# Keys and queries scaled by one instruction each, a chunk's tokens in another order, and x at one place modulo 512 bytes

## The chip, the cores and the metric

The kernel runs on one core of a Trainium2 chip. The metric is the device time of one execution in microseconds (us); lower is better. Engines are named as in the profile: PE is TensorE's matmul, PEld its weight load, DVE VectorE, ACT ScalarE, POOL GpSimd, SP the engine that issues most DMAs.

## The reference

A gated linear attention is followed by two feed-forward layers, all in float32:

```python
# q, k, v, f_logit: (4, 8, 768, 48)
f = 1 / (1 + exp(-f_logit))
for t in range(768):
    state = f[:, :, t, :, None] * state + einsum('bhd,bhe->bhde', k[:, :, t], v[:, :, t])
    y[:, :, t] = einsum('bhd,bhde->bhe', q[:, :, t], state)
x = y.transpose(0, 2, 1, 3).reshape(3072, 384)
h = maximum(x @ w_in1, 0);  x = (h * h) @ w_out1          # 384 -> 2048 -> 384
h = x @ w_in2;  x = where(h > 0, h, exp(minimum(h, 0)) - 1) @ w_out2
```

## The kernel before

**Attention.** The 3072 tokens are 24 groups of 128 (6 chunks of 4 batches; groups 0 to 3 have no carried state). A group's `ff`, `qk` and v tiles hold all 8 heads: two heads on 112 partitions (`ROWS`), four such pairs (`NP`) along the free dimension. `a_decay` makes the products of the gates with two scans on VectorE, outward from the middle of the chunk: `ds[.., 0, ..]` holds the decays of the outward scan, `ds[.., 1, ..]` their counterparts from the scan in the other direction, in runs of 65 elements for each half chunk of 64 tokens. `a_scale` multiplies keys and queries by them, in four instructions of 112x256: each half of the 64-token halves takes its factors from the one or the other scan. The two for k run on GpSimd (L158, L159), the two for q on VectorE (L161, L162), for groups 1 to 3 on GpSimd. Keys lie in the order `outward` (tokens 63 to 0, then 64 to 127), queries in plain order, so one of the four reads its factors backwards. `a_scores` (transposes and scores on TensorE), `a_mask` (VectorE, `copy_predicated` with `msk`), `a_state`, `a_direct` or `a_out` follow, and `a_hi` and `a_lo` write a group's result into x as a rounded part `xh` and a rest `xl`.

**Layers.** Tokens go in 12 blocks of 512, six for each layer (blocks 0 to 5 and 6 to 11), and the 2048 hidden units in 16 slices f. A unit is one (block, slice). `up` makes ph with nine matmuls of 128x512, six with `xh` and three with `xl` (L354). `between` makes gh and gl on ScalarE, VectorE and GpSimd, and `down`, two units later, adds nine matmuls into y (L406), three times gh, gh, gl. So TensorE's order in a unit is xh x6, xl x3, then (gh, gh, gl) x3. Weights of the first layer are decoded from 64-bit words on ScalarE and VectorE (L51, L53, L56, L57) and split in two parts (L323, L324), one slice a unit, ahead of use.

**Order.** Everything is scheduled by hand. `START` lists the first steps, one letter and a number each: f, q, v, r load, g is `a_gate`, d `a_decay`, c `a_scale`, s `a_scores`, t `a_transposed`, m `a_mask`, k `a_state`, y `a_direct`, h `a_hi`, l `a_lo`, w and W decode and split weights, U, B, L are `up`, `between`, `low`. After it the loop over units runs, and `plan` puts the steps of groups 4 to 23 and the weights in front of the `up` of a unit. The steps of a group stand in consecutive units: gate, decay, scale, then scores (block 1) or one unit of pause and scores (later blocks).

**Places.** Pools lie one behind the other in each partition's memory: `one`, `two`, `three`, `wpool`; a pool holds its tags in the order of their first use, each in as many buffers as the pool has (sizes rounded up to 32 bytes). In `two` there are ff, qk, then the two buffers of `xh` and the two of `xl`, then raw, vk, dec, gg, wc, x1; gh, gl and yo are in `three`, the weights in `wpool`. Block 0 takes the second buffer of `xh` and `xl` (the first holds a padded v then), block 1 the first, and so on in turn. An x tile has 3 x 512 + 16 elements, 6208 bytes, and x itself starts 64 bytes into it; 6208 is 64 more than 12 x 512. Tiles of gh, gl (2048 bytes) and weights (6144) are multiples of 512. If r is where xh of the odd blocks starts, modulo 512, then xh of the even blocks starts at r+64, xl of the odd ones at r+128, xl of the even ones at r+192, and gh, gl and the weights, 54,528 bytes behind the first, at r+256.

Of the kernel before, what the change touches and what calls it, by code (L numbers as in the profile page):

```python
# [11 lines left out]
F32 = mybir.dt.float32  # L12
F32R = mybir.dt.float32r
# [17 lines left out]
BLOCKS = [(layer, sum(n[:i]), n[i]) for layer, n in enumerate(SIZES) for i in range(len(n))]  # L31


START = """f0 q0 f1 I q1 M v0 f2 v1 f3 g0 q2 d0 q3 c0 g1 v2 d1 s0 r0 c1 r1 t0 g2 k0 g3 m0 y0 d2 c2 h0 v3 s1 t1
d3 m1 v4 k1 s2 c3 w0 t2 k2 s3 l0 y1 m2 q4 t3 m3 W0 r2 h1 k3 w1 f4 y2 h2 y3 l1
l2 h3 l3 W1 g4 r3 w2 U0 B0 L0 W2 d4 U1 B1 L1 w3 r4"""
FIRST = (0, 3, 6, 8), (-6, -2, 2, 6)
STAGED = 15
DMIN = 2.0**-52


# [18 lines left out]
def chunked(ctx, tc, ff, qk, vk, vz, wraw, mask, ident, flag, out):  # L60
# [8 lines left out]

    one = ctx.enter_context(tc.tile_pool(name="one", bufs=1))  # L70
    two = ctx.enter_context(tc.tile_pool(name="two", bufs=2))
    three = ctx.enter_context(tc.tile_pool(name="three", bufs=3))
    wpool = ctx.enter_context(tc.tile_pool(name="wpool", bufs=NF))
    dram = ctx.enter_context(tc.tile_pool(name="dram", bufs=1, space=bass.MemoryType.DRAM))
# [10 lines left out]
    ss = [one.tile([128, 2, NP, 128], F32, name=f"ss{i}") for i in range(2)]  # L85
    state = [one.tile([ROWS, NP, 48], F32, name=f"state{b}") for b in range(B)]
    dlast = [one.tile([ROWS, NP], F32, name=f"dlast{b}") for b in range(B)]
    x2d = dram.tile([NK, 128, NT], F32, name="x2d")
    wst = dram.tile([NF, 128, 2, 2, DM], F32, name="wst")

# [62 lines left out]
            G.tensor_copy(dlast[g % B], here[:, :, 1])  # L153

    def a_scale(g):
        dt, gt = (ds[g % 2][:, o, o:o + 520].rearrange("r (p h l) -> r p h l", h=2, l=65) for o in range(2))
        q, k = (st[g]["qk"][:, o].rearrange("r (p h l) -> r p h l", h=2, l=64) for o in range(2))
        G.tensor_tensor(out=k[:, :, 0], in0=k[:, :, 0], in1=dt[:, :, 0, 0:64], op=ALU.mult)  # L158
        G.tensor_tensor(out=k[:, :, 1], in0=k[:, :, 1], in1=gt[:, :, 1, 1:65], op=ALU.mult)  # L159
        E = G if 0 < g < B else V  # L160
        E.tensor_tensor(out=q[:, :, 1], in0=q[:, :, 1], in1=dt[:, :, 1, 1:65], op=ALU.mult)  # L161
        E.tensor_tensor(out=q[:, :, 0], in0=q[:, :, 0], in1=gt[:, :, 0, 63::-1], op=ALU.mult)  # L162

    def a_scores(g):
        s = st[g]
# [97 lines left out]

    def new_x(i):
        n = BLOCKS[i][2]
        tiles = [two.tile([128, NK * n + 16], F32R, tag=f"x{p}", name=f"x{p}{i}") for p in "hl"]
        xr[i] = tuple(t[:, 16:].rearrange("r (k t) -> r k t", t=n) for t in tiles)

    def a_hi(g):
        i, o = where[g]  # L270
# [224 lines left out]
def general(ctx, tc, nat, wraw, ident, out):  # L495

    nc = tc.nc
    V, A, G, PE = nc.vector, nc.scalar, nc.gpsimd, nc.tensor
    T = 384
    one = ctx.enter_context(tc.tile_pool(name="g_one", bufs=1))  # L500
    ps = ctx.enter_context(tc.tile_pool(name="g_ps", bufs=1, space=PSUM))
    dram = ctx.enter_context(tc.tile_pool(name="g_dram", bufs=1, space=bass.MemoryType.DRAM))
    yd = dram.tile([2 * B, NP, D, 2, T], F32, name="yd")

    sel = one.tile([ROWS, 2], F32, name="sel")
    vb = one.tile([ROWS, S], F32, name="vb")
    V.memset(sel, 0.0)
    V.memset(sel[0:48, 0:1], 1.0)
    V.memset(sel[64:112, 1:2], 1.0)
    V.memset(vb, 0.0)  # L510
    with tc.For_i(0, B, 1) as b:
        with tc.For_i(0, NP, 1) as p:
            fqk = one.tile([ROWS, 3, S], F32, name="fqk")
            for c in range(3):
                nc.sync.dma_start(out=fqk[:, c], in_=nat[bass.ds(b, 1), bass.ds(p, 1), c].rearrange("b p r s -> (b p r) s"))
            f = fqk[:, 0]
            V.tensor_scalar(out=f, in0=f, scalar1=-80.0, scalar2=None, op0=ALU.max)
            A.activation(f, f, AF.Exp, scale=-1.0)
            V.tensor_scalar(out=f, in0=f, scalar1=1.0, scalar2=None, op0=ALU.add)
            V.reciprocal(out=f, in_=f)  # L520
            with tc.For_i(0, D, 1) as e:
                for j, (lo, hi) in enumerate(HD):
                    src = nat[bass.ds(b, 1), bass.ds(p, 1), 3, bass.ds(e + 64 * j, 1)].rearrange("b p r s -> (b p r) s")
                    nc.sync.dma_start(out=vb[lo:hi], in_=src.to_broadcast([hi - lo, S]))
                kv = one.tile([ROWS, S], F32, name="g_kv")
                V.tensor_tensor(out=kv, in0=fqk[:, 2], in1=vb, op=ALU.mult)
                V.tensor_tensor_scan(out=kv, data0=f, data1=kv, initial=0.0, op0=ALU.mult, op1=ALU.add)
                V.tensor_tensor(out=kv, in0=kv, in1=fqk[:, 1], op=ALU.mult)
                y = one.tile([2, S], F32, name="g_y")
                for h in range(2):  # L530
                    yp = ps.tile([2, T], F32, name=f"g_yp{h}")
                    PE.matmul(yp, sel, kv[:, T * h:T * h + T], start=True, stop=True)
                    A.activation(y[:, T * h:T * h + T], yp, AF.Copy)
                    nc.sync.dma_start(
                        out=yd[bass.ds(2 * b + h, 1), bass.ds(p, 1), bass.ds(e, 1)].rearrange("n p e j t -> (n p e j) t"),
                        in_=y[:, T * h:T * h + T],
                    )
    x = one.tile([128, NK, T], F32, name="g_x")
    acc = one.tile([128, NK, T], F32, name="g_acc")

    with tc.For_i(0, 2, 1) as h, tc.For_i(0, B, 1) as b:
        y = yd[bass.ds(2 * b + h, 1)].rearrange("n p e j t -> (n p) e j t")
        for k in range(NK):
            for j in range(2):
                nc.sync.dma_start(out=x[64 * j:64 * j + 48, k], in_=y[k, :, at_(k, j)])
                nc.sync.dma_start(
                    out=x[64 * j + 48:64 * j + 64, k], in_=y[NP - 1, 16 * k:16 * k + 16, at_(NP - 1, j)]
                )
        for layer in range(2):
            V.memset(acc, 0.0)  # L550
            with tc.For_i(0, NF, 1) as ff:
                raw = one.tile([128, 2 * DM], I64, name=f"g_raw{layer}")
                nc.sync.dma_start(out=raw, in_=wraw[layer, bass.ds(ff, 1)].rearrange("f p m -> (f p) m"))
                w = one.tile([128, 2 * DM], U32, name=f"g_w{layer}")
                decode(nc, raw, w)
                w = w.bitcast(F32)
                ph = ps.tile([128, T], F32, name=f"g_ph{layer}")
                for k in range(NK):
                    PE.matmul(ph, w[:, 128 * k:128 * k + 128], x[:, k], start=(k == 0), stop=(k == NK - 1))
                g = one.tile([128, T], F32, name=f"g_g{layer}")  # L560
                if layer == 0:
                    A.activation(g, ph, AF.Relu)
                    A.activation(g, g, AF.Square)
                else:
                    A.activation(g, ph, AF.Relu, scale=-1.0)
                    th = one.tile([128, T], F32, name="g_t")
                    A.activation(th, g, AF.Tanh, scale=-0.5)
                    A.activation(g, g, AF.Exp, scale=-1.0)
                    V.scalar_tensor_tensor(out=g, in0=g, scalar=1.0, in1=th, op0=ALU.add, op1=ALU.mult)
                    V.scalar_tensor_tensor(out=g, in0=ph, scalar=0.0, in1=g, op0=ALU.max, op1=ALU.add)  # L570
                for m in range(NK):
                    py = ps.tile([128, T], F32, name=f"g_py{m % 2}")
                    PE.matmul(py, w[:, DM + 128 * m:DM + 128 * m + 128], g, start=True, stop=True)
                    V.tensor_tensor(out=acc[:, m], in0=acc[:, m], in1=py, op=ALU.add)
            V.tensor_copy(x, acc)
        for k in range(NK):
            dst = out[k].rearrange("p (h c b t) -> p h c b t", h=2, c=NC // 2, b=B)[:, bass.ds(h, 1), :, bass.ds(b, 1)]
            nc.sync.dma_start(
                out=dst.rearrange("p h c b t -> p (h c b) t"), in_=x[:, k].rearrange("p (c t) -> p c t", t=128)
            )  # L580


# [12 lines left out]
def _layout(q, k, v, f_logit, moe_w_in, moe_w_out, moe2_w_in, moe2_w_out):  # L595
# [9 lines left out]

    ff = np.full((NG, ROWS, 521), -64.0, np.float32)
    ff[:, :, :520].reshape(NG, ROWS, 2 * NP, 65)[:, :, :, 1:] = heads(f_logit, outward, 8.0).reshape(NG, ROWS, 2 * NP, 64)
    qk = np.stack([heads(q, fwd, 0.0), heads(k, outward, 0.0)], axis=2)
    vk = v.reshape(B, NP, 2, NC, 128, D)[:, :, :, :, outward].transpose(3, 0, 4, 1, 2, 5).reshape(NG, 128, DM)
    vz = np.zeros((B, 128, NK, 2, 112), v.dtype)  # L610
    vp = vk[:B].reshape(B, 128, NP, 2, D)
# [18 lines left out]
    for c, a in enumerate((f_logit, q, k, v)):  # L630
        nat[:, :, c, :, :D] = a.reshape(B, NP, 2, S, D).transpose(0, 1, 2, 4, 3)
    nat = nat.reshape(B, NP, 4, 128, S)[:, :, :, :ROWS]
    mask = (outward[:, None] <= fwd[None, :]).astype(np.int32)
    return {
        "ff": ff, "qk": qk, "vk": vk, "vz": vz, "nat": nat, "wraw": wraw, "mask": mask,
        "ident": np.eye(128, dtype=np.float32),
# [14 lines left out]
```

## Time and profile before

| what | value |
|---|---|
| median of 3 timed runs | 930.47 us (927.55 to 930.67) |
| profiled execution, its own time | 927.88 us |
| its span, first to last instruction | 926.1 us |
| mean granted TensorE clock | 0.990 |
| PE busy | 897.8 us (97%) |
| DVE, ACT, POOL busy | 564.7, 441.5, 359.6 us |

The span is what the trace shows; 1.78 us of the execution's time lie outside it. Busy shares are means over stages that differ, so they say which engine is the fullest, not where time can be won.

### The profile page before, as it was taken

The numbers are of one execution on the slowest core, as the hardware profiler recorded it, in microseconds if no ns is written. First come the engines' busy times: TensorE is split into PE (matmuls) and PEld (weight loads), VectorE is DVE, ScalarE is ACT, GpSimd is POOL, SyncE is SP. The second block draws the span as 40 slices with busy tenths as digits, with TensorE's granted clock in tenths as the row PEclk, the third lists the DMA queues.
The fourth block names the chain that finished last, engine by engine and source line by source line (L and its number), as shares of the span: only waits on it lengthen the run. The fifth ranks groups of instructions, "written<-read, shape, count | busy, mean of one in ns | idle before, by whom it ended". The sixth has DMA issues, their size and how long they took to land.

```text
span 926.1 us, 13344 instructions
## 1 busy us (share of the span) xinstructions
PE 897.8 (97%) x5001; PEld 724.5 (78%) x5001; DVE 564.7 (61%) x834; ACT 441.5 (48%) x751; POOL 359.6 (39%) x294
## 2 busy tenths in 40 slices
PE   6798899999999999999999999999999999999996
PEld 4676688878888887777888888888888888888885
DVE  8999977677676776774301356555555565555543
ACT  4477655444444544444444444444444544444443
POOL 5322425555565455553232233233332333323321
PEclk8999999999999999999999999999999999999999
DMA  8456434334344533433256510100100100100001
GB/s 282 143 177 196 134 107 144 109 110 144 111 140 138 189 112 109 145 112 112 103 189 221 201 38 1 57 12 1 58 11 1 57 12 1 57 12 5 31 1 38
DMA packets 30792, 88.46 MB, mean 96 GB/s; under 512 B 4992, under 2 KB 9728, under 8 KB 30720
## 3 DMA queue, kind: packets, MB, share of 16 engines
q1 hardware_dynamic: 28848, 77.32, 25.0%
q10 hardware_dynamic: 1872, 10.22, 3.2%
q8 instruction: 40, 0.66, 0.3%
q14 instruction: 32, 0.26, 0.1%
HBM read 64.52 MB, written 22.02 MB: 93 GB/s over the span
## 4 chain that ended last, share of the span: by engine, by line
PE 89%; DVE 7%; issue 1%; ACT 1%; POOL 1%; DMA 0%; DVEq 0%; ACTq 0%
PE ph L354 42%; PE y L406 41%; PE sc L176 2%; PE o L235 2%; DVE dec L56 1%; PE o L242 1%; DVE ds L140 1%; DVE dec L57 1%; DVE w L324 1%; PE kv L203 1%; DVE dec L53 1%; DVE ss L185 1%; DVE gl L387 1%; PE tp L170 0%; DVE ds L142 0%
## 5 line engine op out<-in xcount | busy, mean ns | idle before, releaser
L393 POOL TENSOR_TENSOR gl<-gg,gh 128x512 fp32r<-128x512 f32 x175 | 245.8, 1405 | 470.5 <-PE ph L354 199.3
L406 PE MATMUL y<-gh,w 128*128 128x512 f32 x576 | 180.0, 394 | 0.0
L406 PE MATMUL y<-gh,wf 128*128 128x512 f32 (+1 forms) x582 | 179.6, 390 | 0.0
L379 DVE SCALAR_TENSOR_TENSOR t<-r,t 128x512 f32<-128x512 f32 (+1 forms) x97 | 71.5, 737 | 162.9 <-ACT r L378 161.8
L354 PE MATMUL ph<-xh,w 128*128 128x512 f32 x576 | 154.5, 403 | 6.9 <-DVE w L324 4.2
L354 PE MATMUL ph<-xh,wf 128*128 128x512 f32 (+1 forms) x582 | 147.8, 389 | 0.0
L375 ACT ACTIVATE r<-ph 128x512 f32<-128x512 f32 (+1 forms) x97 | 57.6, 594 | 186.3 <-PE ph L354 176.9
L354 PEld LDWEIGHTS ph<-xh,w 128*128 128x128 f32 x576 | 105.0, 188 | 35.9 <-DVE w L324 5.4
L406 PEld LDWEIGHTS y<-gh,w 128*128 128x128 f32 x576 | 109.0, 189 | 24.8
L406 PEld LDWEIGHTS y<-gh,wf 128*128 128x128 f32 x582 | 108.9, 188 | 24.3 <-ACT gh L382 0.2
L354 PEld LDWEIGHTS ph<-xh,wf 128*128 128x128 f32 x582 | 108.6, 188 | 23.7
L367 ACT ACTIVATE r<-ph 128x512 f32<-128x512 f32 x96 | 57.1, 595 | 117.5 <-PE ph L354 77.9
L406 PE MATMUL y<-gl,wf 128*128 128x512 f32 (+1 forms) x291 | 112.8, 388 | 0.0
L406 PE MATMUL y<-gl,w 128*128 128x512 f32 x288 | 112.7, 391 | 0.0
L354 PE MATMUL ph<-xl,w 128*128 128x512 f32 x288 | 83.4, 398 | 0.8 <-DVE xl L280 0.8
L354 PE MATMUL ph<-xl,wf 128*128 128x512 f32 (+1 forms) x291 | 82.2, 391 | 0.0
L373 DVE TENSOR_TENSOR gh<-r 128x512 fp32r<-128x512 f32 x64 | 46.0, 718 | 53.4 <-ACT r L367 52.1
L380 DVE SCALAR_TENSOR_TENSOR gg<-ph,t 128x512 f32<-128x512 f32 (+1 forms) x97 | 66.6, 687 | 10.0
L354 PEld LDWEIGHTS ph<-xl,w 128*128 128x128 f32 x288 | 54.7, 190 | 13.4 <-DVE xl L280 1.3
L368 ACT ACTIVATE gg<-r 128x512 f32<-128x512 f32 x96 | 60.7, 633 | 7.7
L406 PEld LDWEIGHTS y<-gl,wf 128*128 128x128 f32 x291 | 54.7, 188 | 12.1 <-DVE gl L387 0.2
L406 PEld LDWEIGHTS y<-gl,w 128*128 128x128 f32 x288 | 54.4, 189 | 12.2
(77 smaller groups left out, 1033.8 us busy)
## 6 DMA issues: line engine op xcount, KB each, us to landing
raw<-wraw SPq DMA_DIRECT2D x19, 768.0 KB, 4.6
wst<-w SPq DMA_DIRECT2D x16, 768.0 KB, 4.3
wf<-wst SPq DMA_DIRECT2D x16, 768.0 KB, 4.3
qk<-qk SPq DMA_DIRECT2D x24, 448.0 KB, 5.8
raw<-wraw ACTq DMA_DIRECT2D x13, 768.0 KB, 4.4
ff<-ff SPq DMA_DIRECT2D x22, 227.9 KB, 4.9
x2d<-yo SPq DMA_DIRECT2D x18, 256.0 KB, 2.2
x<-x2d SPq DMA_DIRECT2D x18, 256.0 KB, 3.2
```

The lines of the kernel that those rows point to most:

```text
L53: V.tensor_scalar(out=out, in0=out, scalar1=3, scalar2=0x7FFFFFFF, op0=ALU.logical_shift_left, op1=ALU.bitwise_and)
L176: PE.matmul(sc[j][:, p], k[lo:hi, p], q[lo:hi, p], start=True, stop=True)
L235: PE.matmul(o[p // 2][r:r + 48, p % 2], s["vk"][:, p, j], ss[g % 2][:, j, p], start=p % 2 == 0, stop=False, skip_group_check=True,)
L354: PE.matmul(ph, w[:, a, 0, 128 * k:128 * k + 128], b[:, k, c], start=(m == 0), stop=(m == len(todo) - 1))
L367: A.activation(r[:, c], ph, AF.Relu)
L368: A.activation(gg[:, c], r[:, c], AF.Square)
L373: V.tensor_tensor(out=gh[:, c], in0=r[:, c], in1=r[:, c], op=ALU.mult)
L375: A.activation(r[:, c], ph, AF.Relu, scale=-1.0)
L379: V.scalar_tensor_tensor(out=t[:, c], in0=r[:, c], scalar=1.0, in1=t[:, c], op0=ALU.add, op1=ALU.mult)
L380: V.scalar_tensor_tensor(out=gg[:, c], in0=ph, scalar=0.0, in1=t[:, c], op0=ALU.max, op1=ALU.add)
L393: G.tensor_tensor(out=gl, in0=gg, in1=gh, op=ALU.subtract)
L406: PE.matmul(yp_[i][m][:, c], w[:, a, 1, 128 * m:128 * m + 128], b[:, c], start=(f == 0 and n_ == 0), stop=(f == NF - 1 and n_ == 2 and c.s ...
```

## The change

- `a_scale` takes one instruction of 512 elements for q and one for k. By its condition k is multiplied on VectorE in all groups, and q on GpSimd in groups 1 to 3, on VectorE otherwise. Its factors are read with one access pattern, which takes one half chunk from the first scan and the other from the second, `apart` elements further on.
- For that the queries of a chunk stand in a new order, `ORDER`: tokens 64 to 127, then 63 to 0. The mask is built for it, x and the output have their tokens in that order, the host puts them back, and `general` (a branch that runs only when a decay is too small) copies its result into that order.
- x tiles lose their 16 unused elements (6144 bytes each). A tile `shift` of 64 bytes that nothing uses stands in the pool `one`, and a pool `gap` with a tile `shift2` of 192 bytes between `two` and `three`.
- `START` has another order of some steps.

```diff
-START = """f0 q0 f1 I q1 M v0 f2 v1 f3 g0 q2 d0 q3 c0 g1 v2 d1 s0 r0 c1 r1 t0 g2 k0 g3 m0 y0 d2 c2 h0 v3 s1 t1
-d3 m1 v4 k1 s2 c3 w0 t2 k2 s3 l0 y1 m2 q4 t3 m3 W0 r2 h1 k3 w1 f4 y2 h2 y3 l1
+START = """f0 q0 f1 I q1 M v0 f2 v1 f3 g0 q2 d0 q3 c0 g1 v2 d1 s0 r0 c1 r1 t0 g2 k0 m0 g3 s1 t1 y0 d2 c2 h0 v3 k1
+m1 s2 d3 v4 t2 y1 c3 k2 m2 s3 h1 w0 t3 l0 y2 k3 m3 W0 r2 h2 q4 w1 y3 f4 l1
 l2 h3 l3 W1 g4 r3 w2 U0 B0 L0 W2 d4 U1 B1 L1 w3 r4"""
+ORDER = np.r_[64:128, 63:-1:-1]
...
+    gap = ctx.enter_context(tc.tile_pool(name="gap", bufs=1))
...
+    one.tile([128, 16], F32, name="shift")
+    gap.tile([128, 48], F32, name="shift2")
...
     def a_scale(g):
-        dt, gt = (ds[g % 2][:, o, o:o + 520].rearrange("r (p h l) -> r p h l", h=2, l=65) for o in range(2))
-        q, k = (st[g]["qk"][:, o].rearrange("r (p h l) -> r p h l", h=2, l=64) for o in range(2))
-        G.tensor_tensor(out=k[:, :, 0], in0=k[:, :, 0], in1=dt[:, :, 0, 0:64], op=ALU.mult)
-        G.tensor_tensor(out=k[:, :, 1], in0=k[:, :, 1], in1=gt[:, :, 1, 1:65], op=ALU.mult)
-        E = G if 0 < g < B else V
-        E.tensor_tensor(out=q[:, :, 1], in0=q[:, :, 1], in1=dt[:, :, 1, 1:65], op=ALU.mult)
-        E.tensor_tensor(out=q[:, :, 0], in0=q[:, :, 0], in1=gt[:, :, 0, 63::-1], op=ALU.mult)
+        a = ds[g % 2]
+        for o, first, apart in ((0, 66, 456), (1, 0, 588)):
+            y = st[g]["qk"][:, o].rearrange("r (p h l) -> r p h l", h=2, l=64)
+            z = bass.AP(a.tensor, a.offset + first, [a.ap[0], [130, NP], [apart, 2], [1, 64]])
+            E = G if o == 0 and 0 < g < B else V
+            E.tensor_tensor(out=y, in0=y, in1=z, op=ALU.mult)
...
-        tiles = [two.tile([128, NK * n + 16], F32R, tag=f"x{p}", name=f"x{p}{i}") for p in "hl"]
-        xr[i] = tuple(t[:, 16:].rearrange("r (k t) -> r k t", t=n) for t in tiles)
+        tiles = [two.tile([128, NK * n], F32R, tag=f"x{p}", name=f"x{p}{i}") for p in "hl"]
+        xr[i] = tuple(t.rearrange("r (k t) -> r k t", t=n) for t in tiles)
...
-    qk = np.stack([heads(q, fwd, 0.0), heads(k, outward, 0.0)], axis=2)
+    qk = np.stack([heads(q, ORDER, 0.0), heads(k, outward, 0.0)], axis=2)
...
-    mask = (outward[:, None] <= fwd[None, :]).astype(np.int32)
+    mask = (outward[:, None] <= ORDER[None, :]).astype(np.int32)
```

## Rows read from the trace of the kernel before

**Rows 1.** The page, part 1: busy time of each engine, its share, instructions.

```profile
PE 897.8 (97%) x5001; PEld 724.5 (78%) x5001; DVE 564.7 (61%) x834; ACT 441.5 (48%) x751; POOL 359.6 (39%) x294
```

**Rows 2.** Table of stretches: length, busy us (instructions), granted clock, DMA share, GB/s.

```profile
32.00:102.00 70.00, 58.84 (x403) 45.04 (x404) 68.20 (x101) 46.51 (x78) 24.30 (x21) 0.98 0.53 172
102.00:447.00 345.00, 345.00 (x2284) 276.61 (x2283) 241.47 (x348) 165.68 (x296) 173.16 (x137) 1.00 0.38 127
...
848.00:918.60 70.60, 70.57 (x324) 58.22 (x322) 34.71 (x57) 32.24 (x55) 20.73 (x16) 1.00 0.03 12
```

**Rows 3.** Chain of waits, 0 to 105 us: shares by line, largest first.

```profile
by line: issue 12.4%; DVE dec L56 10.6%; DVE ds L140 8.8%; DVE dec L57 7.2%; DVE w L324 7.1%; DVE dec L53 5.2%; PE ph L354 5.0%; DVE ss L185 4.8%; DVE gl L387 4.7%; PE sc L176 3.3%; DVE ds L142 2.9%; DMA ff<-ff 2.9%; POOL qk L162 2.8%; POOL
```

**Rows 4.** Chain of waits, 500 to 660 us, in order: start, us, what.

```profile
517.38 2.08 PE ph L354 x9
...
579.48 2.08 PE ph L354 x9
...
585.68 2.07 PE y L406 x9
...
647.48 2.07 PE y L406 x9
```

**Rows 5.** Timeline of TensorE, one unit pair of block 6: start, us, instructions.

```profile
546.20 1.55 PE L354 MATMUL ph<-xh,wf 128*128 128x512 f32 x6
547.59 0.85 PE L354 MATMUL ph<-xl,wf 128*128 128x512 f32 x3
548.28 0.63 PE L406 MATMUL y<-gh,wf 128*128 128x512 f32 x2
...
548.98 0.62 PE L406 MATMUL y<-gh,wf 128*128 128x512 f32 x2
...
549.66 0.62 PE L406 MATMUL y<-gh,wf 128*128 128x512 f32 x2
...
550.34 0.63 PE L354 MATMUL ph<-xh,wf 128*128 128x512 f32 x2
```

**Rows 6.** Timeline of TensorE, one unit pair of block 7.

```profile
612.30 1.52 PE L354 MATMUL ph<-xh,wf 128*128 128x512 f32 x6
613.66 0.86 PE L354 MATMUL ph<-xl,wf 128*128 128x512 f32 x3
614.36 0.63 PE L406 MATMUL y<-gh,wf 128*128 128x512 f32 x2
...
615.05 0.63 PE L406 MATMUL y<-gh,wf 128*128 128x512 f32 x2
...
615.74 0.62 PE L406 MATMUL y<-gh,wf 128*128 128x512 f32 x2
...
616.42 0.39 PE L354 MATMUL ph<-xh,wf 128*128 128x512 f32 x1
```

**Rows 7.** Groups by line and shape, 5 to 102 us: count, busy us, mean ns, idle before.

```profile
L158 POOL TENSOR_TENSOR qk<-qk,ds 112x256 f32<-112x256 f32 x8 | 11.5, 1436 | 0.0
L159 POOL TENSOR_TENSOR qk<-qk,ds 112x256 f32<-112x256 f32 x8 | 8.6, 1076 | 2.4 <-DVE mn L145 2.4
...
L57 DVE SCALAR_TENSOR_TENSOR dec<-raw,dec 128x768 uint32<-128x768 uint32 x13 | 14.3, 1101 | 0.4
...
L161 DVE TENSOR_TENSOR qk<-qk,ds 112x256 f32<-112x256 f32 x5 | 2.1, 410 | 0.0
```

**Rows 8.** Timeline, 70 to 110 us, VectorE and GpSimd.

```profile
80.04 1.33 DVE L56 SCALAR_TENSOR_TENSOR dec<-raw,dec 128x768 uint32<-128x768 uint32 x1
...
80.51 1.41 POOL L159 TENSOR_TENSOR qk<-qk,ds 112x256 f32<-112x256 f32 x1
...
86.35 0.96 DVE L56 SCALAR_TENSOR_TENSOR dec<-raw,dec 128x768 uint32<-128x768 uint32 x1
...
88.22 0.68 DVE L387 TENSOR_TENSOR gl<-gg,gh 128x512 fp32r<-128x512 f32 x1
```

**Rows 9.** Timeline, 30 to 70 us: scores of group 4; in brackets TensorE's idle time.

```profile
47.63 1.16 PE L176 MATMUL sc<-qk 48*128 48x128 f32 x16 [0.97 <-DVE qk L162]
```

More of the change, by code (lines that the diff above doesn't have):

```diff
@@ L575, in general @@
             V.tensor_copy(x, acc)
+        y, z = (a.rearrange("p k (c t) -> p (k c) t", t=128) for a in (acc, x))
+        V.tensor_copy(y[:, :, 0:64], z[:, :, 64:128])
+        V.tensor_copy(y[:, :, 64:128], z[:, :, 63::-1])
         for k in range(NK):
@@ L578, in general @@
             nc.sync.dma_start(
-                out=dst.rearrange("p h c b t -> p (h c b) t"), in_=x[:, k].rearrange("p (c t) -> p c t", t=128)
+                out=dst.rearrange("p h c b t -> p (h c b) t"), in_=acc[:, k].rearrange("p (c t) -> p c t", t=128)
             )
@@ L649 @@
     r = run_bass_kernel_spmd(nc, [arrays], core_ids=[0])
-    return np.ascontiguousarray(r.results[0]["out_t"].reshape(DM, NC, B, 128).transpose(2, 1, 3, 0).reshape(NT, DM))
+    return np.ascontiguousarray(r.results[0]["out_t"].reshape(DM, NC, B, 128)[..., np.argsort(ORDER)].transpose(2, 1, 3, 0).reshape(NT, DM))
```

## The prediction

> **What bounds the kernel now.** I read the page first: TensorE is busy 97% of the span and no other engine more than 61% [rows 1]. A mean hides stages, so the second view is the table of stretches [rows 2]. Up to 102 us VectorE is the full engine (68.20 of 70 us between 32 and 102, TensorE 58.84). From 102 to 447 us TensorE is busy 345.00 of 345 us, and 848 to 918.6 reads the same (70.57 of 70.6). After that come only the last copies and stores. So two clocks set the end: VectorE's sum up to about 102 us, then the plain number of matmuls times what one takes. The third view is the chain of waits of the first stage: it runs through VectorE's decoding (L56, L57, L53, L324) and its scans (L140, L142), not through transfers [rows 3].
>
> The fourth view is the chain in the second layer, where TensorE does nothing but `up` (nine matmuls, ph) and `down` (nine, y). In block 6 sixteen units take (579.48 - 517.38) / 15 = 4.140 us each, in block 7 (647.48 - 585.68) / 15 = 4.120 [rows 4]. Shapes, weights and the other engines' work are the same; what differs is which buffer of `xh` and `xl` the block uses. The fifth view is one such pair from start to start. Block 7 [rows 6]: six xh 612.30 to 613.66 = 1.36, three xl 0.70, then y in threes 0.69, 0.69, 0.68. Block 6 [rows 5]: six xh 1.39, three xl 0.69, y 0.70, 0.68, 0.68. The smallest value per three is 0.68 (0.2267 per matmul), and six xh of block 7 reach it too. Eighteen matmuls at that pace are 6 x 0.68 = 4.08. So an even block loses 0.06 us per pair, an odd one 0.04, and it is lost around the places where the moving tile changes.
>
> **Part 1: where x stands.** From the tile sizes, modulo 512 bytes and with r for xh of odd blocks: xh even r+64, xl odd r+128, xl even r+192; gh, gl and all weights r+256. Set beside the losses: gl to xh in odd blocks (256 bytes apart) costs 0.00; gl to xh in even blocks (192) 0.03; xh to xl (128) 0.02 and 0.01; xl to gh (128 odd, 64 even) 0.02 and 0.02. A switch between tiles at equal residues, as gh to gl, costs nothing once settled. Read modulo 256, every switch with a loss has a distance and the one without has none.
>
> After the change an x tile is 6144 bytes, 12 x 512, so all four buffers stand alike. `shift` moves the pool `two` by 64, which puts them where the 16 unused floats stood: all at r. The tiles behind do not move: +64 - 4 x 64 + 192 = 0, so gh, gl and weights stay at r+256. (The 320 of the title would be an absolute place; the argument needs only distances.) Then xh to xl is a switch of 0, and the other two are of 256, the distance that costs 0.00 in block 7. The pair falls to 4.08. Between 102 us and the end lie blocks 1 to 11: 5 even ones, 80 pairs x 0.06 = 4.8 us, and 6 odd ones, 96 x 0.04 = 3.8: together 8.6. The last three units of block 0 would add 0.2; left out. Bounds: half of the 80 pairs of blocks 1 to 5 are interrupted by attention matmuls, and if the 16 of them in even blocks keep the 0.03 at xh, 0.5 is missing: 8.1. Nothing at all is the other end, if the place is not the cause. The Trainium skill, page "SBUF — State Buffer", section "SBUF: two separate sides", says that TensorE has ports of its own and never waits for another engine; by that rule the place of x changes nothing and this term is 0. The 4.140 beside 4.120 of one and the same work disagree.
>
> **Part 2: one multiplication for two, and keys on VectorE.** The four instructions of 256 elements become two of 512, and the condition in `a_scale` puts them elsewhere: k, which GpSimd multiplied for all 24 groups, is VectorE's now, and GpSimd keeps q of groups 1 to 3 alone. From 102 us on TensorE waits for neither engine and VectorE works 241 of 345 us [rows 2], so this costs and gives nothing there; its cover is the plan, which calls `a_scale` two units ahead of `a_scores` in later blocks, and a unit takes over 4.1 us [rows 4]. With that cover gone each of the 16 groups from 8 on would hand its delay to TensorE.
>
> Before 102 us VectorE is the clock, and groups 0 to 7 fall there. *Added:* an instruction of 512 elements like gl's takes 0.68 [rows 8], one of q's two 0.41 [rows 7]. Groups 0 and 4 to 7 go from 2 x 0.41 to 2 x 0.68, +0.54 each; groups 1 to 3 get k, +0.68 each: 5 x 0.54 + 3 x 0.68 = 4.7 us. *Removed:* GpSimd ran 22 multiplications here, 8 + 8 of k [rows 7] and 6 of q. One that meets VectorE slows it: decoding L56 takes 1.33 beside L159 and 0.96 alone [rows 8]. 19 instructions fewer, at 0.37 at most, are 7.0 us. The least that went this way is seen in L57, which averages 1.10 over 13 instances [rows 7] and with L56, its like, loses 26 x 0.14 = 3.6. The three q instructions left are twice as long and may cost 0.7 each instead of 2 x 0.37: the same. So the sum lies between 1.1 us lost and 2.3 gained. I take 1.0 gained, nearer the upper end, since scans, gl and the small products meet GpSimd too.
>
> The new order of waits: k was multiplied on GpSimd right behind the scans, a unit before q. Now it stands behind q in VectorE's queue, and TensorE's transposes of k, ahead of the scores, wait for it. At group 4 the scores already waited 0.97 for q [rows 9]. They would start later by k's 0.68 and by the transposes, which take less than the 1.16 of the 16 scores: 0.7 to 1.8 us. Behind them on TensorE stand the next `up` and `down`; for these wait ScalarE and then VectorE's gl. I take 0, because VectorE, not TensorE, sets this stage and has decoding to do meanwhile; what it costs if VectorE does wait is rival D.
>
> **Part 3: the order of the start.** Masks m1 and m2 move ahead of d3 and w0 on VectorE, s1 and t1 ahead of y0 on TensorE and ScalarE, k1 and k2 earlier, h1 ahead of w0 on ScalarE, W0 and w1 keep their place. SP's queue changes in one place, raw block 2 ahead of q4, which is used only at c4, behind the first two units. Apart from part 2 VectorE executes the same instructions, one pair of mask instructions earlier and d3 that much later. As VectorE is full anyway (idle 1.8 of 70 us), an order can win only idle time: 0 to 1, I take 0.
>
> **Part 4.** The columns of queries and the mask are permuted on the host: same bytes, same instructions. The two copies added in `general` lie in a branch that isn't taken: 0.
>
> **Sum.** The profiled execution took 927.88: span 926.10 and 1.78 around it. 926.10 - 8.6 - 1.0 = 916.5, plus 1.78 is 918.3. The three timed runs (927.55, 930.47, 930.67) and this one average 929.1, the median is 930.47; the same 9.6 off the mean of the four gives 919.5, which I forecast for the median after. What a measurement here tells from no change is about 0.5%, 4.65 us.
>
> **Rivals.**
> A. *As summed*: 918.3 to 920.9 (1.0% faster). Chance 0.54.
> B. *The switch back still costs.* The free switch by 256 bytes is seen in one direction, gl to xh; xl to gh may keep its 0.02. Then 80 x 0.04 + 96 x 0.02 = 5.1 and the 1.0 are gained: 921.8 from the profiled run, 924.4 from the median. For it: the loss in y appears with every xl before it, whether 64 or 128 away. Against: in both it was a distance modulo 256. Chance 0.17.
> C. *It does not do what it says.* Nobody writes `shift` or `shift2`. If the allocator gives unused tiles no room, x stands at r-64 and all behind it 256 lower, at r: two switches of 64, which cost 0.02 to 0.03 each, as much as now; or the place of x is not the cause at all. Time 926.9 to 929.5. The page named above would have it so too. Against: two tiles of one buffer pair differ in nothing but place. Chance 0.12.
> D. *VectorE waits for late scores.* Masks of groups 4 to 7 wait for the scores, and all of VectorE's queue behind them: four times 0.7 to 1.8 us, 2.8 to 7.2 in the stage where VectorE is the clock. 918.3 + 5.0 = 923.3 from the profiled run, 925.9 from the median. For it: groups 4 to 7 have no unit of pause between scale and scores. Against: VectorE has over 3 us of decoding a unit to do in between. Chance 0.12.
> E. *Slower.* The loss of a switch grows with its distance: 0.02 at 64, 0.03 at 192, so 0.04 at 256, in both directions now and in every pair: 0.08 instead of 0.06 and 0.04, that is 80 x 0.02 + 96 x 0.04 = 5.4 us more, less 1.0: 932.3 to 934.9. Nothing is gained any more from (8.6 + 1.0) / (2 x 176) = 0.027 a switch. Against it stands block 7, whose switch by 256 costs nothing. Chance 0.05.
>
> **Numbers.** A, most of B and a quarter of D are faster by over 0.5%: 0.72; C and the rest of B and D: 0.23; E: 0.05. The range 916.0 to 927.0 takes in A with a start up to 2.3 us better, B, D and the edge of C, and leaves out E, most of C and a start better still, about 0.19. The likeliest case's own range is 916.0 to 921.5.
>
> **What the profile will show.** Right: pairs of 4.08 in all blocks of the second layer, the same in even and odd ones; six xh in 1.36 and xl in 0.68 everywhere; the full stage still beginning at about 102 us. B: xh and xl at pace, but the first y of a pair at 0.70. C: 4.14 and 4.12 as before. D: TensorE's full stage begins 3 to 7 us later, with VectorE idle ahead of masks. E: pairs above 4.14, lost at xh and at the first y. Part 2 shows in VectorE's qk rows: two of about 0.7 us in each group, L56 and L57 at 0.96, and GpSimd's qk rows gone but for three. Wrong altogether would be a stage after 102 us in which TensorE waits for qk.

## The result, and the profile after

The changed kernel takes **919.39 us** (median of 6 runs, 917.56 to 921.72) beside 929.51 us for the kernel before (6 runs, 927.55 to 930.67): ratio 0.9896, 95% interval 0.9874 to 0.9918. The forecast median was 919.5. The profiled execution took 917.91 us, with a span of 916.1 us at a mean granted clock of 0.990; the span of before was 926.1.

The page, part 1, and below it the stretches that answer to [rows 1] and [rows 2]:

```profile
PE 890.3 (97%) x5001; PEld 724.5 (79%) x5001; DVE 562.4 (61%) x837; ACT 440.8 (48%) x751; POOL 295.2 (32%) x243
```

```profile
32.00:102.00 70.00, 59.47 (x402) 45.48 (x402) 67.27 (x100) 46.49 (x78) 9.23 (x13) 0.95 0.57 179
102.00:437.00 335.00, 333.98 (x2252) 269.50 (x2251) 237.81 (x342) 162.06 (x290) 130.68 (x104) 1.00 0.39 130
```

The same 5001 matmuls take TensorE 7.5 us less. VectorE, the clock of the first stage, has 67.27 us of work from 32 to 102 us where it had 68.20. TensorE's granted clock reads 0.95 there, before 0.98. From 102 to 437 us TensorE is full again but for 1.02 us (335 - 333.98).

The chain of waits in the second layer, to set beside [rows 4]:

```profile
512.94 2.04 PE ph L360 x9
514.98 2.04 PE y L412 x9
...
578.22 2.04 PE ph L360 x9
...
639.42 2.04 PE ph L360 x9
```

Sixteen units of block 6 take (578.22 - 512.94) / 16 = 4.08 us each, and fifteen of block 7 (639.42 - 578.22) / 15 = 4.08: the even and the odd block no longer differ. The timeline of TensorE shows inside a pair what [rows 5] and [rows 6] showed; ahead of it stand two rows that later paragraphs use:

```profile
113.58 1.21 PE L360 MATMUL ph<-xh,w 128*128 128x512 f32 x4 [1.02 <-DVE w L330]
...
129.77 1.52 PE L360 MATMUL ph<-xh,w 128*128 128x512 f32 x6
...
541.34 1.52 PE L360 MATMUL ph<-xh,wf 128*128 128x512 f32 x6
542.70 0.84 PE L360 MATMUL ph<-xl,wf 128*128 128x512 f32 x3
543.38 0.61 PE L412 MATMUL y<-gh,wf 128*128 128x512 f32 x2
...
544.06 0.61 PE L412 MATMUL y<-gh,wf 128*128 128x512 f32 x2
...
544.74 0.61 PE L412 MATMUL y<-gh,wf 128*128 128x512 f32 x2
...
545.42 0.84 PE L360 MATMUL ph<-xh,wf 128*128 128x512 f32 x3
...
606.62 1.52 PE L360 MATMUL ph<-xh,wf 128*128 128x512 f32 x6
607.98 0.84 PE L360 MATMUL ph<-xl,wf 128*128 128x512 f32 x3
```

From start to start block 6 now reads 1.36, 0.68, 0.68, 0.68, 0.68, and block 7 begins the same way.

**Where the 10.0 us of span came from.** Three rows of the kernel before and two of the changed one mark the pieces: the first `up` of block 1, the first of block 6 and the last matmul of the last `down` (the changed kernel's 129.77 stands above).

```profile
130.83 1.52 PE L354 MATMUL ph<-xh,w 128*128 128x512 f32 x6
...
517.22 1.55 PE L354 MATMUL ph<-xh,wf 128*128 128x512 f32 x6
...
918.29 0.28 PE L406 MATMUL y<-gl,wf 128*128 128x256 f32 x1
...
512.78 1.52 PE L360 MATMUL ph<-xh,wf 128*128 128x512 f32 x6
...
909.12 0.28 PE L412 MATMUL y<-gl,wf 128*128 128x256 f32 x1
```

The first `up` of block 1 starts at 129.77 us; before it was 130.83: 1.06. The first `up` of block 6 starts 383.01 us later; before it was 386.39: 3.38. From there to the start of the last matmul it is 396.34 against 401.07: 4.73. What follows it, above all the last copies and stores, is shorter by about 0.8, which nobody forecast; in the other profiled runs that end took from 6.9 to 8.4 us, so this is not shown to come from the change. 1.06 + 3.38 + 4.73 + 0.8 = 10.0.

The first of these terms is not shown by the two traces alone. The runs `e3_x_places` and `e4_xl_places` below have the same first stage as the changed kernel, with x of blocks 0 to 5 at the same places modulo 512, and their block 1 begins at 130.87 and 130.62 us: single traces of one and the same stage lie 1.1 us apart. (The granted clock from 100 to 110 us reads 1.00 in the changed kernel, 0.67 and 0.83 in these two.) So a start of block 1 that differs by 1 us between two traces settles nothing below; the times do, where they are clear.

VectorE's and GpSimd's groups by line and shape, 5 to 102 us, to set beside [rows 7]:

```profile
L58 DVE SCALAR_TENSOR_TENSOR dec<-raw,dec 128x768 uint32<-128x768 uint32 x13 | 13.1, 1004 | 0.4
L57 DVE SCALAR_TENSOR_TENSOR dec<-raw,dec 128x768 uint32<-128x768 uint32 x13 | 12.5, 958 | 0.5
...
L168 DVE TENSOR_TENSOR qk<-qk,ds 112x512 f32<-112x512 f32 x13 | 8.7, 698 | 0.0
L147 DVE TENSOR_TENSOR_SCAN ds<-ff,lim 112x521 f32<-112x521 f32 x6 | 7.5, 1244 | 0.2
...
L393 DVE TENSOR_TENSOR gl<-gg,gh 128x512 fp32r<-128x512 f32 x10 | 7.3, 725 | 0.0
...
L168 POOL TENSOR_TENSOR qk<-qk,ds 112x512 f32<-112x512 f32 x3 | 5.1, 1691 | 4.0 <-DVE mn L150 4.0
```

The decoding takes 0.958 and 1.004 instead of 1.10 twice, gl 0.725 instead of 0.810, and all scans 1.24 (before, four of the means of such groups ran from 1.241 to 1.629). The price is the 8.7 us of keys and queries, where VectorE had 4.7 us of queries.

### The profile page after: what moved, and what is told of

It is laid out like the page before. It is cut to its first block, busy times and chain, and to the rows that moved or that the text cites. A ratio compares the mean times of both kernels' runs of the same rounds, so it can differ in the third digit from the quotient of the medians.

```text
span 916.1 us, 13300 instructions
## 1 busy us (share of the span) xinstructions
PE 890.3 (97%) x5001; PEld 724.5 (79%) x5001; DVE 562.4 (61%) x837; ACT 440.8 (48%) x751; POOL 295.2 (32%) x243
## 4 chain that ended last, share of the span: by engine, by line
PE 92%; DVE 4%; DMA 1%; issue 1%; ACT 1%; SPq 0%; DVEq 0%
PE ph L360 42%; PE y L412 42%; PE sc L182 3%; PE o L241 2%; PE o L248 1%; DMA ff<-ff 1%; PE kv L209 1%; PE tp L176 1%; DVE ds L145 1%; DVE dec L57 1%; DVE w L330 0%; DVE qk L168 0%; PE yp L226 0%; DVE dec L58 0%; DVE gl L393 0%
## 5 line engine op out<-in xcount | busy, mean ns | idle before, releaser
L399 POOL TENSOR_TENSOR gl<-gg,gh 128x512 fp32r<-128x512 f32 x175 | 250.0, 1429 | 500.1 <-PE ph L360 192.2
L412 PE MATMUL y<-gh,w 128*128 128x512 f32 x576 | 177.4, 389 | 0.0
L360 PEld LDWEIGHTS ph<-xl,wf 128*128 128x128 f32 x291 | 54.4, 188 | 11.1
```

The lines of the kernel that those rows point to most:

```text
L360: PE.matmul(ph, w[:, a, 0, 128 * k:128 * k + 128], b[:, k, c], start=(m == 0), stop=(m == len(todo) - 1))
L399: G.tensor_tensor(out=gl, in0=gg, in1=gh, op=ALU.subtract)
L412: PE.matmul(yp_[i][m][:, c], w[:, a, 1, 128 * m:128 * m + 128], b[:, c], start=(f == 0 and n_ == 0), stop=(f == NF - 1 and n_ == 2 and c.s ...
```

## The experiments

The theories. **M**, the prediction's: a *switch* between moving tiles costs when their places differ by no multiple of 256 bytes. **W**, formed after the first results: what counts is the distance, modulo 256, between the tile that streams and the *weights*. For the first stage: VectorE's gain comes from GpSimd's instructions leaving, against the rival that it comes from the new START. Places below are in bytes.

**1 and 2. The two halves apart.** `e1_x_only` is the kernel before with only the x tiles, `shift` and `gap`; `e2_scale_only` is the changed kernel with the old x tiles and without them.

```diff
-        tiles = [two.tile([128, NK * n + 16], F32R, tag=f"x{p}", name=f"x{p}{i}") for p in "hl"]
-        xr[i] = tuple(t[:, 16:].rearrange("r (k t) -> r k t", t=n) for t in tiles)
+        tiles = [two.tile([128, NK * n], F32R, tag=f"x{p}", name=f"x{p}{i}") for p in "hl"]
+        xr[i] = tuple(t.rearrange("r (k t) -> r k t", t=n) for t in tiles)
```

> The kernel before with the places of x alone changed: x tiles without the 16 elements, shift and shift2, nothing else. Theory (places of the moving tiles): every unit pair of the second layer takes 4.08 us, in even and odd blocks, and the time falls by 8.6 us, about 920.9 where before has 929.5 (ratio 0.991). Rival (the gain came from scaling and the order of the start): pairs of 4.14 and 4.12 as before and no change of time.

> The changed kernel with x back at its four old places: scaling by one instruction, keys on VectorE, the tokens' order and the order of the start stay. Theory: pairs of 4.14 and 4.12 as before, and 1.0 to 1.5 us less from the start, about 928.3 (ratio 0.9985). Rival: the stage ahead of 102 us gives 3 us or more, or loses, since keys come later to TensorE: 926 or 931.

Measured: x alone 920.19 us (919.08 to 922.44), ratio 0.9912 (0.9898 to 0.9926), all pairs of the second layer 4.08. The rest alone 926.73 us (925.52 to 927.93), ratio 0.9976 (0.9965 to 0.9987), pairs 4.14 and 4.12 as before. Block 1 begins at 130.66 with x alone (before 130.83) and at 129.70 with the rest alone. So the place of x is worth about 8 us (8.2 by the ratio, 8.8 by the medians). The rest is a small gain, 1.2 to 3.3 us by the interval of its ratio; its trace begins block 1 1.1 us earlier, which alone would show nothing. On top of the place of x it can't be told from nothing: the intervals of e1 and of the changed kernel (0.9874 to 0.9918) overlap.

**3 and 4. Which distance costs.** Tiles of x in the changed kernel get 128 elements more, and each block of the second layer its own offset in them: in `e3_x_places` the same for xh and xl, in `e4_xl_places` for xl alone, while xh stays at gh's place.

```diff
-        tiles = [two.tile([128, NK * n], F32R, tag=f"x{p}", name=f"x{p}{i}") for p in "hl"]
-        xr[i] = tuple(t.rearrange("r (k t) -> r k t", t=n) for t in tiles)
+        at = PLACE[i]
+        tiles = [two.tile([128, NK * n + 128], F32R, tag=f"x{p}", name=f"x{p}{i}") for p in "hl"]
+        xr[i] = tuple(
+            t[:, o:o + NK * n].rearrange("r (k t) -> r k t", t=n) for t, o in zip(tiles, at)
+        )
```

> The changed kernel with x tiles 512 bytes longer and x at another place in each block of the second layer, xh and xl alike: 0, 64, 128, 192, 32 and 16 bytes from gh and gl modulo 512 in blocks 6 to 11 (blocks 0 to 5 at 256 as in the changed kernel). Theory (a switch of the moving tile costs when its distance is not a multiple of 256 bytes): 4.08 us a pair at 0, about 4.13 at 64 and 192, 4.12 at 128, and 4.09 to 4.11 at 32 and 16. Rival 1 (it is enough that xh and xl stand alike): 4.08 to 4.09 in all six. Rival 2 (what counts is the bare distance, growing): 4.08 at 0, then 4.09, 4.10, 4.11 for 16, 32, 64 and up to 4.14 for 192.

> As the run before, with xh always at the place of gh and xl at 256, 64, 128, 192, 32 and 448 bytes from it modulo 512 in blocks 6 to 11. Theory (distance modulo 256): 4.08 us a pair at 256, though xh and xl stand 256 bytes apart; 4.12 to 4.14 at 64, 128, 192 and 448, 448 like 192; about 4.10 at 32. Rival (xh and xl must stand alike): 4.10 or more at 256 too.

Measured, the time of a pair (ten pairs of each block), by the distance from gh, which here is also that from the weights:

| distance, bytes | 0 | 256 | 64 | 128 | 192 | 32 | 16 | 448 |
|---|---|---|---|---|---|---|---|---|
| e3: xh and xl | 4.08 | | 4.147 | 4.16 | 4.16 | 4.18 | 4.167 | |
| e4: xl alone | | 4.08 | 4.153 | 4.12 | 4.12 | 4.127 | | 4.12 |

The whole runs took 925.58 and 922.48 us, one execution each. 256 is as free as 0, also when xh and xl differ by it: only the distance modulo 256 counts, and the tiles need not stand alike modulo 512. But the expected sizes were missed (4.09 to 4.13 in e3; in e4 4.12 to 4.14 at 64 and 4.10 at 32): the losses are larger, in e3 largest at the small distance of 32, and at 64 moving xl alone costs as much as moving both. In block 6 of e3 (distance 0) six xh and three xl average 1.36 and 0.68, as in the changed kernel. TensorE's timeline in block 9 (192):

```profile
745.35 1.56 PE L364 MATMUL ph<-xh,wf 128*128 128x512 f32 x6
746.75 0.86 PE L364 MATMUL ph<-xl,wf 128*128 128x512 f32 x3
747.45 0.62 PE L416 MATMUL y<-gh,wf 128*128 128x512 f32 x2
...
748.14 0.62 PE L416 MATMUL y<-gh,wf 128*128 128x512 f32 x2
...
748.83 0.61 PE L416 MATMUL y<-gh,wf 128*128 128x512 f32 x2
```

In block 9 the six xh take 1.40 and the three xl 0.70, that is 0.233 for every one of the nine, though xh and xl stand alike and nothing is switched between them. The y behind them take 0.69, 0.69, 0.68: they need some matmuls to come back. A price for each switch cannot do that; theory M is in doubt, and W is formed.

Block 7 (distance 64), two threes of y and the `up` behind them, shows what W does not explain:

```profile
610.96 0.62 PE L416 MATMUL y<-gh,wf 128*128 128x512 f32 x2
...
611.65 0.62 PE L416 MATMUL y<-gh,wf 128*128 128x512 f32 x2
...
612.34 1.54 PE L364 MATMUL ph<-xh,wf 128*128 128x512 f32 x6
613.72 0.85 PE L364 MATMUL ph<-xl,wf 128*128 128x512 f32 x3
614.40 0.63 PE L416 MATMUL y<-gh,wf 128*128 128x512 f32 x2
```

Here the badly placed xh and xl lose little (1.38 and 0.68), and the well placed y take 0.69 each and do not come back: over eleven pairs the three of a unit average 0.698, 0.690 and 0.697. How the loss is shared between a badly placed tile and the well placed ones behind it changes with the distance, and why stays open.

**5. The weights moved.** `e5_w_moved` puts the weights 128 bytes further on, so that gh and the weights differ, and gives each block of the second layer a place of x.

```diff
+PLACE = [(0, 0), (0, 0), (0, 0), (0, 0), (0, 0), (0, 0), (64, 64), (96, 96), (32, 32), (80, 80), (112, 112), (0, 0)]
...
+    gap3 = ctx.enter_context(tc.tile_pool(name="gap3", bufs=1))
     wpool = ctx.enter_context(tc.tile_pool(name="wpool", bufs=NF))
...
+    gap3.tile([128, 32], F32, name="shift3")
```

> The changed kernel with all weights moved by 128 bytes against gh and gl, and x at 0, 128, 384, 64, 192 and 256 bytes from gh in blocks 6 to 11 (so at -128, 0, 256, -64, 64 and 128 from the weights). Theory M (what costs is the switch between moving tiles): 4.08 us a pair in blocks 6 and 11, where all moving tiles stand alike modulo 256, and 4.12 or more in the others. Theory W (what costs is the distance between the tile a matmul streams and the weights loaded meanwhile): the nine of up at pace (2.04) in blocks 7 and 8, where x stands with the weights, and slow (2.06 to 2.10) elsewhere, and the nine of down slow (about 2.10) in every block; so 4.14 in blocks 7 and 8 and up to 4.20 in blocks 6 and 11, and blocks 0 to 5 slower than in the changed kernel.

Measured (935.03 us in one execution; slower than the kernel before): with x at 0, 128, 384, 64, 192 and 256 from gh the pairs take 4.20, 4.16, 4.16, 4.187, 4.163 and 4.183. Block 6 is the test: there all moving tiles stand alike (distance 0 from each other), and only the weights are 128 away. By M it takes 4.08; it takes 4.20. TensorE's timeline, block 6 and block 7:

```profile
554.44 1.56 PE L366 MATMUL ph<-xh,wf 128*128 128x512 f32 x6
555.84 0.86 PE L366 MATMUL ph<-xl,wf 128*128 128x512 f32 x3
556.54 0.63 PE L418 MATMUL y<-gh,wf 128*128 128x512 f32 x2
...
557.24 0.63 PE L418 MATMUL y<-gh,wf 128*128 128x512 f32 x2
...
621.31 1.55 PE L366 MATMUL ph<-xh,wf 128*128 128x512 f32 x6
622.70 0.84 PE L366 MATMUL ph<-xl,wf 128*128 128x512 f32 x3
623.38 0.62 PE L418 MATMUL y<-gh,wf 128*128 128x512 f32 x2
...
624.07 0.63 PE L418 MATMUL y<-gh,wf 128*128 128x512 f32 x2
```

In block 6 every three matmuls take 0.70, in both halves. In block 7 x stands with the weights again: `up` comes to 0.68 at xl, and the loss is in `down` (0.69, then 0.70). The chain of waits says the same in whole pieces: `up` 2.07 and `down` 2.09, where block 8 of e3, with x at that same place but the weights with gh, has `up` 2.09 and `down` 2.07. What was slow went over from the one to the other when the weights moved. That the weights' new place is slow by itself is excluded by the xl of block 7, which use the same weights and take 0.68. M falls; of W the reference stands, the weights. Its sizes were missed here too: for blocks 7 and 8 it said 4.14, with `up` at 2.04, and blocks 6 and 11, equal by any distance modulo 256, take 4.20 and 4.183. Blocks 1 to 5 came out slower, as it said (391.22 us from the first `up` of block 1 to that of block 6, in the changed kernel 383.01). That a matmul streams its tile while weights are loaded beside it (PEld is busy 79% of the span) makes a meeting of these two reads the likely mechanism; that is argued, not shown.

**6. The old START.** `e6_old_start` is the changed kernel with the three lines of START of before.

> The changed kernel with START of the kernel before. Theory (an order cannot win where VectorE is full): no difference to the changed kernel, 919.4, and block 1 of TensorE begins at 129.8 us within 0.3. Rival (the earlier start comes from the order): block 1 begins 1 us later, 920.4.

Measured: 918.79 us (917.26 to 918.96), ratio 0.9877 (0.9861 to 0.9892), block 1 at 130.13 (changed kernel 129.77). The order moves block 1 by 0.36 us, less than such traces differ by, and nothing shows in the times.

**7. Keys back on GpSimd,** in one instruction: `e7_k_gpsimd`.

```diff
-            E = G if o == 0 and 0 < g < B else V
+            E = G if o == 1 or 0 < g < B else V
```

> The changed kernel with k multiplied by one instruction on GpSimd in all groups. Theory (the start gains because GpSimd leaves VectorE alone): L57 and L58 back at 1.10 us mean in the first 102 us, VectorE's sum there not smaller though it does less, block 1 begins about 1 us later than in the changed kernel, 920.4. Rival (one instruction instead of two is what gains): as the changed kernel, or better by VectorE's 8 x 0.6 us.

Measured: 922.93 us (920.36 to 924.88), ratio 0.993 (0.9915 to 0.9945); block 1 at 131.72. Groups of 5 to 102 us:

```profile
L168 POOL TENSOR_TENSOR qk<-qk,ds 112x512 f32<-112x512 f32 x11 | 17.7, 1616 | 6.0 <-DVE mn L150 5.4 <-issue 0.6
L57 DVE SCALAR_TENSOR_TENSOR dec<-raw,dec 128x768 uint32<-128x768 uint32 x13 | 16.0, 1227 | 0.5
```

L57 takes 1.227 instead of 0.958: 13 x 0.27 = 3.5 us of VectorE's time for 8 keys that GpSimd multiplies. L58 takes 0.983, so both together average 1.11, as before the change (1.10), and VectorE's sum from 32 to 102 us is 67.86 us, not less than the changed kernel's 67.27: as the theory said. Block 1 is 1.95 us later than in the changed kernel, more than the 1.1 by which such traces differ, and the intervals of the two ratios only just meet. So the runs speak for the theory, that what gains is the keys' leaving GpSimd and not the joining of instructions.

**8. gl of block 0 on GpSimd too.** If GpSimd's instructions cost little, moving VectorE's sixteen gl of the first stage would gain: `e8_gl_gpsimd`.

```diff
-            if (i, f) == final or i == 0:
+            if (i, f) == final:
...
-        if (i, f) != final and i > 0:
+        if (i, f) != final:
```

> The changed kernel with gl of block 0 computed on GpSimd, as in later blocks, instead of on VectorE. VectorE has 16 x 0.68 us less to do in the stage where it is the clock; GpSimd is nearly idle there. Theory: each GpSimd instruction of 1.3 us takes at least 0.4 and at most 1.3 us from VectorE where the two meet, so the gain is between +4 and -10 us; 0.4 is seen more often for short ones, so about 3 us gained, 916. Rival: at 1 us each nothing or a loss, 919 to 925.

Measured: 925.33 us (922.36 to 926.54), ratio 0.9945 (0.9928 to 0.9962); block 1 at 137.44, 7.7 us later than in the changed kernel.

```profile
L58 DVE SCALAR_TENSOR_TENSOR dec<-raw,dec 128x768 uint32<-128x768 uint32 x12 | 17.4, 1452 | 0.4
...
63.81 0.96 DVE L57 SCALAR_TENSOR_TENSOR dec<-raw,dec 128x768 uint32<-128x768 uint32 x1
64.29 1.62 POOL L399 TENSOR_TENSOR gl<-gg,gh 128x512 fp32r<-128x512 f32 x1 [1.94 <-ACT gh L377]
64.80 1.93 DVE L58 SCALAR_TENSOR_TENSOR dec<-raw,dec 128x768 uint32<-128x768 uint32 x1
```

L58, one of the decoding's steps, goes from 1.004 to 1.452. VectorE lost 16 x 0.68 us of work and still came 7.7 us later: (7.7 + 10.9) / 16 = 1.16 us at most for one GpSimd instruction, waits for its result included.

The three timeline rows show which instruction pays. L57 was running when GpSimd's gl began, and kept its 0.96; L58 began while that gl ran, and took 1.93. So it is in the traces of before, the changed kernel, e7 and e8 from 30 to 110 us: of 31 instructions (the decoding's last two steps and gl) that VectorE began during a GpSimd instruction of over 0.5 us, 30 took longer than alone (the exception began 0.03 us behind it); those that were running when GpSimd's began did not.

**9 and 10. GpSimd emptied further.** `e9_q_vector` multiplies the queries of groups 1 to 3 on VectorE too; `e10_gate_scalar` also takes the second step of the gate of groups 4 to 7 from GpSimd to ScalarE.

```diff
-            E = G if o == 0 and 0 < g < B else V
-            E.tensor_tensor(out=y, in0=y, in1=z, op=ALU.mult)
+            V.tensor_tensor(out=y, in0=y, in1=z, op=ALU.mult)
...
-        if g < B:
+        if g < 2 * B:
             A.activation(f, f, AF.Copy, scale=0.5, bias=0.5)
```

> The changed kernel with q of groups 1 to 3 multiplied on VectorE too, so that GpSimd multiplies nothing. VectorE gets 3 x 0.68 = 2.0 us more and loses three meetings with GpSimd instructions of 1.3 us. Theory (a GpSimd instruction takes from VectorE nearly its own length where they meet, as gl on GpSimd showed): 3 x 1.2 = 3.6 less, block 1 begins 1 to 1.6 us earlier than the 129.8 of the changed kernel. Rival (at the start VectorE waits for other things when GpSimd multiplies q): 0 to 2 us later.

> The run before, and besides the second step of the gate of groups 4 to 7 on ScalarE instead of GpSimd. VectorE loses four or five meetings with instructions of 0.64 us, ScalarE gets five of 0.64. Theory: up to 5 x 0.5 = 2 us less on VectorE, block 1 begins 0.5 to 2 us earlier than in the run before, the best of all versions at 917 to 918. Rival (ScalarE, which stands between TensorE and VectorE, is delayed, or those instructions met little): no difference.

Measured: e9 920.58 us (920.2 to 921.79), ratio 0.9902 (0.9887 to 0.9917), block 1 at 131.79, 2.0 us later than in the changed kernel. e10 920.88 us (920.48 to 922.93), ratio 0.9903 (0.9888 to 0.9918), block 1 at 132.90. Neither gains. For e9 the timeline of the changed kernel, around the query of group 2, shows why:

```profile
12.11 0.69 DVE L168 TENSOR_TENSOR qk<-qk,ds 112x512 f32<-112x512 f32 x1
12.15 1.69 POOL L168 TENSOR_TENSOR qk<-qk,ds 112x512 f32<-112x512 f32 x1 [1.35 <-DVE mn L150]
14.21 1.24 DVE L145 TENSOR_TENSOR_SCAN ds<-f,lim 112x520 f32<-112x520 f32 x1
```

GpSimd's 1.69 us end before VectorE's next scan begins. What lies beside them is the key's multiplication (0.69) and a mask (1.34 for two); in e9, with nothing beside them, two multiplications take 1.29 and the mask 1.34. So that query cost VectorE nothing: the key's multiplication was running when it began. Moving it delays the next scan by 0.62 (14.83 instead of 14.21), and behind the third query the first step of the decoding comes at 25.57 instead of 24.01: 1.56 of the 2.0 us. The granted clock from 10 to 15 us also reads 0.50 in e9 and 0.62 in the changed kernel. That e10 comes another 1.1 us later is no more than such traces differ by (its clock from 100 to 110 us reads 0.66, in e9 1.00).

No version of these runs beats the changed kernel. By their intervals e1, e6, e9 and e10 can't be told from it; e8 is slower, and e7 very likely.

## Why the prediction was right, and which step of it failed

**The sum held, term by term.** x: 8.6 forecast, bound 8.1 with interrupted pairs; 3.38 + 4.73 = 8.1 measured. Blocks 6 to 11 gave 4.7 of the 4.8 that 48 x 0.06 + 48 x 0.04 make, blocks 1 to 5 3.4 of 3.8; that interrupted pairs are why was not tested. a_scale: 1.0 taken, between -1.1 and 2.3; the traces read 1.06, no more than two traces of one stage differ by; e2's ratio gives 1.2 to 3.3 us, START included. That it gains is shown, how much only within these bounds. START and the host's order: 0 forecast; nothing that the times can tell. Rival A it was.

**The step that failed is Part 1's reason,** "it is lost around the places where the moving tile changes" and a price for each switch by its distance. The rows it stood on were the first matmuls behind a switch ([rows 5], [rows 6]), and in the kernel before gh and the weights stood at one place, so "distance from gh" and "distance from the weights" were the same number. In its place e3 and e5 show: time is lost when a tile streams at another place than the weights, modulo 256 bytes, and not at a switch. At 128 and 192 bytes all nine of `up` lose, and the first well placed ones behind them some still; at 64 the well placed ones lose most. The xl of [rows 6] fits: at r+128, 128 from the weights, three took 0.70 beside xh at r with 0.227 each. The number came out because the change puts x at r and the weights at r+256, which is right under both readings: as far as the reason goes, luck. A change that lined up x with gh while the weights stand elsewhere would have been forecast as a gain, and e5's block 6 shows a loss of 0.12 a pair.

**The rivals.** B (the switch back costs) and E (loss grows with distance) are refuted by the pairs of 4.08, and E's rule by 4.18 at 32 bytes beside 4.16 at 128 and 192. C is refuted by e1: ratio 0.9912 from the place alone. By the Trainium skill, page "SBUF — State Buffer", section "SBUF: two separate sides", TensorE never waits for another engine, and as the prediction read that rule this part would give 0. The runs do not contradict the rule: here it is TensorE's own pace that changes with the place (4.08 against 4.14 and 4.12 a pair). D's wait is there, without its price: the chain of waits of the changed kernel at group 4 reads

```profile
46.27 1.22 DVE qk L168 x2
47.48 0.04 issue
47.53 0.60 PE tp L176 x4
48.13 1.43 PE sc L182 x16
```

The transposes wait 3.06 us for the key (L168); the scores start at 48.13, before at 47.63 [rows 9], 0.5 later where 0.7 to 1.8 were forecast. VectorE meanwhile decodes and is busy 4.93 of the 5 us from 45 to 50 and from 50 to 55, as before.

**Part 2's terms.** Added work was forecast at 4.7 us; the rows of 5 to 102 us show 8.7 - 4.7 = 4.0 on VectorE. Contention removed was bounded by 3.6 and 7.0; the groups show 3.1 in L56 and L57, 1.5 in the scans, 0.8 in gl, and 0.4 and 0.9 in two small ones (L53: 588 to 554 ns, the minimum behind the scans, L145: 255 to 147): 6.7. That is 2.7 more than was added; VectorE's busy time, in which overlapping rows count once, fell by 1.6 (94.03 to 92.40 us). One reading was off: the L56 of 1.33 in [rows 8] was put beside L159, but it began at 80.04 while L158 still ran, from 78.55 to 80.55, and L57 after it met L159.

**What was not foreseen.** At 113.58 us TensorE waits 1.02 us for VectorE's split of weights (L330). So it does in e1, e7 and e9, and not in before, e2, e6, e8 and e10. That x is well placed, and TensorE so comes to the last slices of block 0 earlier, can't be the whole reason: e6 and e10 have x at the same places and no such wait. The cause stays open. The wait for qk after 102 us, named as what would be wrong altogether, did not come.

## What to carry to other kernels

When TensorE is full and one matmul's pace differs between buffers of the same tile, compare the buffers' byte places with those of the weights modulo 256, and line up every moving tile with the weights, not only with each other. While VectorE is the clock of a stage, a GpSimd instruction is priced by what it slows on VectorE and not by GpSimd's idle time: look at which VectorE instruction begins while it runs before moving work in either direction. Before a difference of 1 us between two traces is read as a gain, look at what two traces of an unchanged stage differ by. When two references coincide in the kernel before (here gh and the weights), no row of it can tell which one counts.

## What the runs showed of the hardware that was not expected

- Eighteen matmuls of 128x512 take 4.08 us with tiles and weights at one place modulo 256 bytes, and 4.12 to 4.20 otherwise. At its best a matmul takes 0.2267, badly placed at 128 or 192 bytes 0.233. A distance of 32 bytes (4.18) costs more than 64 (4.147). Why 256 was not found out.
- At 128 and 192 bytes the loss doesn't settle while the place is wrong, and needs some matmuls to go when it is right again (0.70, 0.69, 0.68 for threes of y in block 8 of e3). At 64 it doesn't go within the nine of `down` (0.698, 0.690, 0.697).
- What a GpSimd instruction costs VectorE depends on which begins first: a step of the decoding that began while gl ran on GpSimd took 1.93, one that was running already kept its 0.96 (e8). It depends on the kind too: masks (1.34 for two) and, but for one case of 0.92 in before, the decoding's first step (0.55) that began during one were hardly longer than alone.
